# Moving the result matmuls to the head of the values loop, and halving the last quarters on VectorE, in a decode-attention kernel

## The chip, the cores and the metric

The kernel runs on one core of a Trainium2 chip. The metric is the device time in microseconds (us) of one execution. Most runs of one kernel agree within a few tenths of a microsecond. Kernels are compared only within the same rounds. A "ratio" is the mean time of one kernel's fast runs over the mean of the other's fast runs of the same rounds, so it is not quite the ratio of the medians quoted beside it.

## The reference

```python
B, H, Sq, Skv, Dh = 8, 32, 1, 4096, 128          # q, k, v in bf16
scores = jnp.einsum('bhqd,bhkd->bhqk', q, k) * Dh ** -0.5
attn = jax.nn.softmax(scores, axis=-1)
out = jnp.einsum('bhqk,bhkd->bhqd', attn, v)
```

There are 256 heads with one query each. K and V are 268 MB each and every byte is used once. A tile is 8 heads: 128 partitions by 256 rows of 128 numbers, 8.39 MB. There are 32 tiles of K and 32 of V.

## The kernel before

For each tile t, VectorE multiplies K by the query and adds halves of the 128 columns together; TensorE adds up the columns that are left (matmuls with the identity), VectorE reduces the result to scores. ScalarE makes the weights. TensorE multiplies them with V in a loop one section later. The values of a tile stand in 32 rows and are picked out by four small matmuls ("result matmuls") and scaled.

```python
C, NT = 256, 32                     # rows per partition and tile; tiles
def width_of(t, lo):                # columns left for TensorE
    return D // 8 if lo == C // 2 and 0 < t < NT - 3 else D // 2

def product(t, lo, hi):
    # multiply by q, then, while more than width_of(t, lo) columns: add halves
...
def values_loop(t):
    with tc.tile_critical() as loop:           # TensorE alone, a While loop
        for i in range(EDGE):
            one(i, start=(i == 0), stop=False)
        ...                                    # 10 rounds of 6 matmuls
        for i in range(NV - EDGE, NV):
            one(i, start=False, stop=(i == NV - 1))
...
for t in range(NT):
    loop = 0 < t <= LT                         # LT = NT - 3 = 29
    ...
    product(t, 0, first)
    if 0 < t - 1 <= LT:
        if (t - 1) % R == 0:
            norm_of(n)
        if t > 1:
            result_of(t - 2)                   # four matmuls
    if t + 2 < NT:
        q_prep(t + 2)
    if loop:
        sum_over_d(t, 0, HALF)
        product(t, HALF, C)
        sum_over_d(t, HALF, C)
        scores_of(t, 0, HALF)
        ...
        values_loop(t - 1)
        load("k", t + 1)
        load("v", t)
        scores_of(t, HALF, C)
    else:
        ...                                    # quarters instead of halves
```

K and V share three buffers. K of tile t+1 takes the buffer that the loop over V of tile t-2 leaves; V of tile t takes the buffer of K of tile t once its sums are done. So the end of a loop releases the next issue of K, and the end of the sums the next issue of V.

## Time and profile before

| | before |
|---|---|
| median of 3 runs | 1250.9 us (1250.84 to 1250.91) |
| span of the profiled run | 1249.5 us |
| DMA queue of K and V, share of the span | 99.5% |
| VectorE busy | 81% |
| TensorE busy | 61% |
| time from one landing to the next, mid-run | 19.35 us for 8.39 MB |

How to read it: no compute engine is full and the queue is. The lines are in the prediction, with what each shows.

### The profile page before, as it was taken

The numbers are of one execution on the slowest core, as the hardware profiler recorded it, in microseconds if no ns is written. First come the engines' busy times: TensorE is split into PE (matmuls) and PEld (weight loads), VectorE is DVE, ScalarE is ACT, GpSimd is POOL, SyncE is SP. The second block draws the span as 40 slices with busy tenths as digits, with TensorE's granted clock in tenths as the row PEclk, the third lists the DMA queues.
The fourth block names the chain that finished last, engine by engine and source line by source line (L and its number), as shares of the span: only waits on it lengthen the run. The fifth ranks groups of instructions, "written<-read, shape, count | busy, mean of one in ns | idle before, by whom it ended". The sixth has DMA issues, their size and how long they took to land. (4 is left out here: it accounts for less than half of the span.)

```text
span 1249.5 us, 10534 instructions
## 1 busy us (share of the span) xinstructions
PE 761.4 (61%) x3004; PEld 284.3 (23%) x3004; DVE 1010.6 (81%) x379; ACT 166.1 (13%) x433; POOL 4.5 (0%) x24
## 2 busy tenths in 40 slices
PE   3356457554586555766557665577655676556855
PEld 1122122221222212222122222122221222212312
DVE  7877987778977789777797777987779877798694
ACT  0111011111011110111101111011110111101111
POOL 1000000000000000000000000000000000000000
PEclk9786798777887777878678777887867877778867
DMA  9999999999999999999999999999999999999998
GB/s 405 436 436 435 436 429 424 426 436 437 436 432 435 435 434 434 435 435 426 431 436 435 426 430 436 435 434 437 433 432 430 433 437 432 433 432 425 429 442 339
DMA packets 11430, 537.30 MB, mean 430 GB/s; under 512 B 1808, under 2 KB 2064, under 8 KB 2320
## 3 DMA queue, kind: packets, MB, share of 16 engines
q1 hardware_dynamic: 11072, 536.94, 99.5%
q8 instruction: 14, 0.23, 0.1%
q10 hardware_dynamic: 336, 0.07, 0.0%
q14 instruction: 8, 0.07, 0.0%
HBM read 536.94 MB, written 0.07 MB: 430 GB/s over the span
## 5 line engine op out<-in xcount | busy, mean ns | idle before, releaser
L189 DVE TENSOR_TENSOR kt<-kt,qb 128x16384 bf16<-128x16384 bf16 (+1 forms) x70 | 556.8, 7955 | 156.8 <-DMA kt<-in_k_dram 150.1
L207 PE MATMUL ps<-kt,ident 128*128 128x512 bf16 x688 | 253.2, 537 | 416.3 <-DVE kt L195 415.9
L290 PE MATMUL av<-vt,w 128*32 x1740 | 425.3, 397 | 4.4
L195 DVE TENSOR_TENSOR kt<-kt 128x4096 bf16<-128x4096 bf16 (+1 forms) x126 | 382.7, 3037 | 4.3
L290 PEld LDWEIGHTS av<-vt,w 128*32 x1740 | 173.3, 100 | 262.1 <-issue 118.9
L207 PEld LDWEIGHTS <-ident 128*128 128x128 bf16 x688 | 80.0, 125 | 583.0 <-DVE kt L195 444.7
L244 ACT ACTIVATE e<-sc,nmax 128x256 bf16<-128x256 f32 x32 | 16.2, 508 | 708.0 <-DVE nmax L238 708.0
L251 ACT ACTIVATE w<-e,mine 128x256 bf16<-128x256 bf16 x256 | 105.6, 495 | 1.1
L219 DVE TENSOR_REDUCE sc<-ps 128x128 f32<-128x512 f32 (+1 forms) x70 | 48.1, 687 | 57.0 <-PE ps L207 57.0
L347 ACT ACTIVATE comb<-av 32x512 bf16<-32x512 f32 (+1 forms) x32 | 18.8, 586 | 327.3 <-PEq L280 320.9
L276 PE MATMUL av<-vt,w 128*32 128x512 bf16 x116 | 47.1, 498 | 14.5 <-issue 13.3
L367 PE MATMUL op<-comb,pick 32*16 32x128 bf16 (+1 forms) x128 | 12.2, 213 | 21.9 <-ACT comb L347 21.9
L276 PEld LDWEIGHTS av<-vt,w 128*32 128x32 bf16 x116 | 6.9, 101 | 54.7 <-issue 54.7
L175 PE MATMUL qp<-qg,heads 8*128 8x128 bf16 x32 | 7.0, 217 | 16.7 <-ACT qg L173 16.7
L367 PEld LDWEIGHTS <-pick 32*16 32x16 bf16 (+1 forms) x128 | 8.7, 83 | 28.9 <-issue 28.5
L231 DVE TENSOR_REDUCE pmax<-sc 128x1 f32<-128x256 f32 x32 | 13.4, 420 | 1.1
L318 PE MATMUL av<-vt,w 128*32 128x512 bf16 x188 | 13.7, 417 | 0.0
L173 ACT ACTIVATE qg<-qh 8x128 bf16<-8x128 f32 x32 | 8.5, 267 | 33.5 <-PE qh L169 33.5
L169 PE MATMUL qh<-q_all,ident 128*8 128x128 bf16 x32 | 7.2, 225 | 8.7 <-DMA q_all<-in_q_dram 8.3
L177 ACT ACTIVATE qb<-qp 128x128 bf16<-128x128 f32 x32 | 8.9, 278 | 9.7 <-PE qp L175 9.7
L339 DVE RECIPROCAL rz<-zp 16x1 f32<-16x1 f32 x16 | 2.3, 147 | 8.1 <-PE zp L332 8.1
L233 DVE TENSOR_SCALAR spread<-same,pmax 128x32 f32<-128x32 f32 x32 | 7.7, 242 | 1.1
(30 smaller groups left out, 45.7 us busy)
## 6 DMA issues: line engine op xcount, KB each, us to landing
kt<-in_k_dram SPq DMA_DIRECT2D x4, 4096.0 KB, 23.8
kt<-in_k_dram SPq DMA_DIRECT2D x4, 2048.0 KB, 12.3
vt<-in_v_dram SPq DMA_DIRECT2D x1, 4096.0 KB, 33.1
vt<-in_v_dram SPq DMA_DIRECT2D x1, 2048.0 KB, 37.6
vt<-in_v_dram SPq DMA_DIRECT2D x1, 1024.0 KB, 39.7
vt<-in_v_dram SPq DMA_DIRECT2D x1, 512.0 KB, 40.5
vt<-in_v_dram SPq DMA_DIRECT2D x31, 26.2
kt<-in_k_dram SPq DMA_DIRECT2D x29, 28.7
```

What stands on the lines that cost most here:

```text
L189: nc.vector.tensor_tensor(out=part, in0=part, in1=qb[:].to_broadcast([P, hi - lo, D]), op=ALU.mult)
L195: nc.vector.tensor_tensor(out=part[:, :, 0:n], in0=part[:, :, 0:n], in1=part[:, :, n : 2 * n], op=ALU.add)
L207: nc.tensor.matmul(ps[:], lhsT=ident[:], rhs=kt[:, lo:hi, s * ds : (s + 1) * ds], start=(s == 0), stop=(s == n - 1),)
L219: made = nc.vector.tensor_reduce(out=scs[t][:, lo:hi], in_=ps, axis=AX.X, op=ALU.add)
L231: nc.vector.tensor_reduce(out=pmax[:], in_=sc[:], axis=AX.X, op=ALU.max)
L244: nc.scalar.activation(out=e[:], in_=sc[:], func=ACT.Exp, bias=nmax[:, 0:1], scale=scale, accum_out=esums[t // R][:, t % R : t % R + 1],)
L251: nc.scalar.activation(out=w[:, :, g, :], in_=e_g, func=ACT.Copy, scale=mine[:, 0, g : g + 1])
L276: pe.matmul(av, lhsT=wf[:, i * nw : (i + 1) * nw], rhs=vf[:, i * nv : (i + 1) * nv], **how)
L290: pe.matmul(av, lhsT=wf[:, bass.ds(ow + i * nw, nw)], rhs=vf[:, bass.ds(ov + i * nv, nv)], start=False, stop=False,)
L318: nc.tensor.matmul(avs[t][j * AG : (j + 1) * AG, :], lhsT=w[:, i, :, :], rhs=vt[:, c0 : c0 + CB, :], start=(i < TG), stop=(j not in group[ ...
L347: nc.scalar.activation(out=comb[0:n, :, :], in_=av[0:n, :, :], func=ACT.Copy)
L367: nc.tensor.matmul(ops[n][:], lhsT=pick[0:e, m, r, :], rhs=comb[0:e, m, :], start=(r == 0 and m == 0), stop=(r == R - 1 and m == CB - 1 an ...
```

## The change

The intent: take TensorE work and a wait from in front of the first-half sums, and make the last tiles' scores come sooner by giving their last quarters' additions to VectorE.

```diff
+    LT = NT - 3
 ...
     def width_of(t, lo):
-        return D // 8 if lo == C // 2 and 0 < t < NT - 3 else D // 2
+        if t == 0:
+            return D // 2
+        return D // 8 if lo == (C // 2 if t <= LT else 3 * C // 4) else D // 2
 ...
         with tc.tile_critical() as loop:
+            if t > 0:
+                result_of(t - 1)
             for i in range(EDGE):
                 one(i, start=(i == 0), stop=False)
 ...
                 if (t - 1) % R == 0:
                     norm_of(n)
-                if t > 1:
+                if t > LT:
                     result_of(t - 2)
```

The rest of the diff renames a variable and moves `LT` up.

More of the change, by code (lines that the diff above doesn't have):

```diff
@@ L299, in values_loop @@
         loops.append(loop)
-    LT = NT - 3
     def values_of(t, lo, hi):
@@ L397 @@
         for t in range(NT):
-            loop = 0 < t <= LT
+            halves = 0 < t <= LT
             v_last = t >= NT - 2
             n = t // R - 1
-            if not loop:
+            if not halves:
                 if t + 1 < NT:
@@ L404 @@
                 load("v", t)
-            first = HALF if loop else Q
+            first = HALF if halves else Q
             product(t, 0, first)
-            if not loop:
+            if not halves:
                 sum_over_d(t, 0, first)
@@ L415 @@
                 q_prep(t + 2)
-            if loop:
+            if halves:
                 sum_over_d(t, 0, HALF)
@@ L440 @@
                 values_of(t - 1, 0, C)
-            if not loop:
+            if not halves:
                 scores_of(t, HALF + Q, C)
@@ L449 @@
                     store_of(n)
-                if not loop:
+                if not halves:
                     if t % R == 0:
```

## The prediction

> **What bounds the kernel now.** I read the busy shares first, then the DMA rows, then the waits, then one tile in the middle of the timeline, and last the end of the program. From the page:
>
> ```profile
> PE 761.4 (61%) x3004; PEld 284.3 (23%) x3004; DVE 1010.6 (81%) x379; ACT 166.1 (13%) x433; POOL 4.5 (0%) x24
> DMA  9999999999999999999999999999999999999998
> q1 hardware_dynamic: 11072, 536.94, 99.5%
> L189 DVE TENSOR_TENSOR kt<-kt,qb 128x16384 bf16<-128x16384 bf16 (+1 forms) x70 | 556.8, 7955 | 156.8 <-DMA kt<-in_k_dram 150.1
> vt<-in_v_dram SPq DMA_DIRECT2D x31, 26.2
> kt<-in_k_dram SPq DMA_DIRECT2D x29, 28.7
> ```
>
> No compute engine is full: VectorE, the busiest, is at 81%, and 150.1 us of its idle time is waiting for a K tile. The queue that carries K and V is busy 99.5% of the span. So the transfer is the suspect, and the question is whether it ever runs dry. One tile of the timeline answers that (start, duration, instruction):
>
> ```profile
> 618.16 0.33 SPq L156 DMA_DIRECT2D vt<-in_v_dram  x1
> 619.39 14.81 PE L290 MATMUL av<-vt,w 128*32 x60
> 625.12 8.69 DVE L189 TENSOR_TENSOR kt<-kt,qb 128x16384 bf16<-128x16384 bf16 x1 [5.29 <-DMA kt<-in_k_dram]
> 635.03 0.33 SPq L156 DMA_DIRECT2D kt<-in_k_dram  x1
> 635.67 0.38 PE L367 MATMUL op<-comb,pick 32*16 32x128 bf16 x4 [0.81 <-ACT comb L347]
> 638.33 5.32 PE L207 MATMUL ps<-kt,ident 128*128 128x512 bf16 x16 [1.57 <-DVE kt L195]
> ```
>
> A K tile lands just before 625.12, when VectorE's wait ends. The V tile was issued at 618.16, so 7 us before that; with the median of 26.2 us it lands at 644.4. The next K tile was issued at 635.03, which is 9.3 us before V lands; with its 28.7 us it lands at 663.7. So landings are at about 625.0, 644.4, 663.7: one each 19.35 us, and each transfer is queued 7 to 9 us before its predecessor is done. One tile is 128 x 256 x 128 x 2 bytes = 8.39 MB, and 8.39 MB / 19.35 us = 434 GB/s. The window of that period shows the same (last three numbers: TensorE clock, DMA share, GB/s):
>
> ```profile
> 625.00:663.70 38.70, 24.11 (x95) 9.15 (x94) 31.83 (x11) 5.03 (x13) 0.00 (x0) 0.78 1.00 434
> ```
>
> 64 such tiles at 19.35 us are 1238.4 us. The rest of 1249.5 is [...] some slower tiles, and what follows the last bytes.
>
> **The end.** The chain that ended last has V's transfer until 1245.48; then:
>
> ```profile
> 1242.30 3.09 PE L318 MATMUL av<-vt,w 128*32 128x512 bf16 x28
> 1245.53 0.83 PE L359 MATMUL op<-vt,w_last 128*16 128x128 bf16 x12
> 1246.19 0.39 PE L367 MATMUL op<-comb,pick 128*16 128x128 bf16 x4
> 1246.42 0.39 PE L359 MATMUL op<-vt,w_last 128*16 128x128 bf16 x4
> 1246.84 0.36 ACT L378 ACTIVATE stage<-op,rz 16x128 bf16<-16x128 f32 x1 [0.73 <-PE op L359]
> 1242.50:1245.00 2.50, 2.50 (x27) 1.05 (x26) 0.13 (x1) 0.00 (x0) 0.00 (x0) 0.81 0.60 224
> 1245.00:1247.50 2.50, 1.67 (x25) 1.18 (x20) 0.00 (x0) 0.96 (x2) 0.00 (x0) 1.00 0.11 39
> ```
>
> The first of the twelve at 1245.53 answers the landing of the eight-row piece of V at 1245.48, though the values matmuls before it had only just ended (1245.39). From there twenty small matmuls run without a gap, at (0.83 - 0.22) / 11 = 56 ns from one to the next (0.22 is the mean of one in the groups by line).
>
> [...] the trace swings between 0.50 and 1.00, and weight loads of the 512-column sums follow each other at 0.43 us in half-clock stretches.
>
> **The change part by part.** *A, result matmuls.* The order of instructions shows 28 groups of four (tiles 0 to 27) taken from in front of the query preparation and put in front of the values loop of the same section. Removed: a wait for the copy (16.6 us in all for 29 groups, about 0.6 each) and 0.38 us, per tile, between the loop's end and the first-half sums. These sums wait 1.57 us for VectorE anyway (the L207 row above), so taking some 1 us from in front of them moves nothing. Added: four 128-column matmuls before the loop, 4 x 56 ns = 0.22 us at full clock, or some 0.43 at half. The loop ends 0.2 to 0.4 us later, and so does the K issue that waits for it. Its 9.3 us of lead becomes about 9.0. V's issue waits for the sums, not the loop: unchanged. In odd sections the stage activation now also waits for the loop's end and stands before the copy there: +0.34 us on the copy and the query preparation after it, inside the same 1.57 us of slack together with the 1 us gained. Effect on the span: 0.
>
> *B, halving.* The diff's new width rule touches three tiles, not two. Tile 29 (the third last): its second half gets two more VectorE halvings, 2.29 + 1.23 = 3.5 us, and loses 12 of 16 sums at 0.43 = 5.1 us. V of tile 29 is issued about 1.5 us earlier than 1162.25. Tiles 30 and 31: the last quarter gets halvings of 2048 and 1024 elements, 1.23 + about 0.69 (estimate: 2292 - 1225 = 1067 ns for 2048 elements, so 1225 - 533) = 1.9 us, and loses 6 of 8 sums at 0.43 = 2.6 us. Net gain about 0.7 each. Summed with tile 29's, less A's 0.3: 1.5 + 0.7 + 0.7 - 0.3, so tile 31's last scores (1232.69) come about 2 us earlier (estimate, 1 to 2.5), and its first values at 1239.23 become some 1237.3. But V's pieces land when they land. The later value groups then wait for their pieces, and the twelve still begin at the 1245.48 landing. After it nothing is shorter: 12 + 4 + 4 matmuls, 0.36 us, the store. Effect: 0. Total VectorE +7.3 us, TensorE about -10 us, span 0.
>
> **The rivals.** *All hidden* (my choice): 1250.9. For it: every transfer has 6 us or more of lead, and the end is set by a landing. *The tail's clock falls back.* The values of tile 31 will come earlier and with holes between V's pieces, [...] twenty matmuls at 107 instead of 56 ns are +1.0 us: 1251.9. For it: the windows show 0.81 in the stretch just before, so it became full only there. [...] *The tail gains.* Values end earlier, so the copy at 1245.51 comes earlier: but the four that need it stand behind the twelve in TensorE's order and never waited for it. At most 0.2 us: 1250.7. *A new wait starves the DMA*: the loop would have to be over 9 us late, or V over 6; A adds 0.4 us. If it did by 1 us per tile, 28 us: 1279. I see no path. *Removed waits speed the middle*: only if transfers had gaps there; the 434 GB/s says not.
>
> **Range and chances.** Nothing in the middle moves; the tail gives -0.2 to +1.0. The three runs before lie within 0.07 us, but another chip or day may differ by some tenths (the profiled run took 1251.34). I take 1250.9, range 1250.1 to 1252.0. Over 2% would be 25 us either way: there is no such path down (it would need a faster DMA), and up only by starvation. Chances 0.005, 0.99, 0.005.
>
> **What would show each step right or wrong.** K issues with about 9 us lead, V with about 7, still 19.35 us per landing and 434 GB/s; the K wait of VectorE near 150 us; L367 gone from the place after the copy; VectorE's busy time +7, tile 31's last score some 2 us earlier, idle holes of TensorE between the last values; the end again V's landing, then some 1.3 us of matmuls. Wrong: a DMA share under 0.95 in mid-span windows, a granted clock of 0.5 after 1245 (then +1), or last values ending before and the twelve starting before V's piece has landed (impossible by the chain above).

The marked cuts are passages that no trace or run of this case shows. The forecast's sum is 1250.9 us (the median before) with 0 for part A and 0 for part B. In the rival of the falling clock the +1.0 us stands as an estimate: 20 x (107 - 56) ns, where 107 is a quarter of the 0.43 us by which weight loads of the 512-column sums follow each other at a granted clock of 0.50 (561.33 to 563.89 in the trace before; at 1.00, from 564.27, seven take 1.40 us). A clock that falls in a pause is seen in that trace too: TensorE's sums end at 643.65, the next start at 654.98, and the granted clock is 1.00 in the window from 643.65 to 646.13 and 0.50 from 646.13 to 654.97. Of the start the trace shows that the first packet of K comes at 1.82 us.

## More of the kernel before

The page lists queues 8 and 14 too, as of the kind `instruction`:

```profile
q8 instruction: 14, 0.23, 0.1%
q14 instruction: 8, 0.07, 0.0%
```

The columns are packets, MB and the share of the 16 DMA engines' time. Such a packet is called an instruction fetch below.

## The result, and the profile after

| | before | after |
|---|---|---|
| median of 6 runs each | 1250.9 us (1250.77 to 1251.86) | 1251.51 us (1251.27 to 1252.11) |
| ratio | | 1.0004, interval 0.9991 to 1.0017 |
| span of the profiled run | 1249.5 us | 1249.7 us |

The time is the same, as predicted, and within the range. Yet five of six runs before lie at or under 1250.91, and all six after at or over 1251.27: there is a small thing of about 0.6 us that the prediction has at 0.

The page after, busy times and the queue of instructions:

```profile
PE 744.1 (60%) x2980; PEld 288.4 (23%) x2980; DVE 1017.9 (81%) x385; ACT 163.2 (13%) x433; POOL 4.4 (0%) x24
q14 instruction: 9, 0.07, 0.0%
```

VectorE has six instructions and 7.3 us more, TensorE 24 fewer matmuls. And there is one packet of queue 14 more. One tile in the middle of the timeline after (start, duration, instruction):

```profile
617.78 0.33 SPq L157 DMA_DIRECT2D vt<-in_v_dram  x1
618.20 0.59 PE L370 MATMUL op<-comb,pick 32*16 32x128 bf16 x4 [0.45 <-issue]
618.72 1.03 PE L279 MATMUL av<-vt,w 128*32 128x512 bf16 x2
624.76 8.69 DVE L191 TENSOR_TENSOR kt<-kt,qb 128x16384 bf16<-128x16384 bf16 x1 [5.30 <-DMA kt<-in_k_dram]
635.01 0.33 SPq L157 DMA_DIRECT2D kt<-in_k_dram  x1
637.97 3.63 PE L209 MATMUL ps<-kt,ident 128*128 128x512 bf16 x16 [1.70 <-DVE kt L197]
```

The result matmuls now stand at 618.20, in front of the loop, which starts 0.52 us later (618.72 less 618.20). The first-half sums still wait for VectorE, 1.70 us instead of 1.57. VectorE still waits 5.3 us for K. Nothing in the middle moved, and the window of the same stretch gives the same rate:

```profile
625.00:663.70 38.70, 22.55 (x94) 9.12 (x93) 31.83 (x12) 5.17 (x14) 0.00 (x0) 0.82 1.00 434
```

The end of the timeline after, from TensorE's values of tile 31 on, and the windows there (clock, DMA share and GB/s at the right):

```profile
1241.40 1.89 PE L321 MATMUL av<-vt,w 128*32 128x512 bf16 x16 [2.28 <-DMA vt<-in_v_dram]
1243.88 0.61 PE L321 MATMUL av<-vt,w 128*32 128x512 bf16 x8 [0.59 <-DMA vt<-in_v_dram]
1245.10 0.40 PE L321 MATMUL av<-vt,w 128*32 128x512 bf16 x4 [0.61 <-DMA vt<-in_v_dram]
1245.75 0.83 PE L362 MATMUL op<-vt,w_last 128*16 128x128 bf16 x12 [0.25 <-DMA vt<-in_v_dram]
...
1247.06 0.36 ACT L381 ACTIVATE stage<-op,rz 16x128 bf16<-16x128 f32 x1 [0.86 <-PE op L362]
1242.50:1245.00 2.50, 1.41 (x15) 0.48 (x11) 0.00 (x0) 0.00 (x0) 0.00 (x0) 1.00 0.51 193
1245.00:1247.50 2.50, 1.68 (x24) 1.19 (x23) 0.00 (x0) 0.96 (x2) 0.00 (x0) 1.00 0.06 17
```

Where 28 values matmuls ran as one stretch before, each group now waits for its piece of V: the scores came sooner and the gain became waiting. The end is again a landing: the eight-row piece landed at 1245.71, and the twelve start at 1245.75. Before, that piece landed at 1245.48. So what came later is V itself, by 0.23 us in this pair of traces. (The profiled run of the kernel before took 1251.34 us, 0.4 more than its median, and its K of tile 31 landed late, as the next paragraph shows. That hides part of the difference in this pair.)

Following the landings back (issue plus time to landing), one transfer stands out. K of tile 31 landed at 1207.04 before and 1206.59 after. V of tile 30, which follows it in the queue, was issued at 1199.45 before and 1197.78 after. Its time to landing, from the view of that instruction, before and then after:

```profile
DMA to landing us min/median/max: 27.0/27.0/27.0
```

```profile
DMA to landing us min/median/max: 28.9/28.9/28.9
```

It landed at 1226.44 and at 1226.71: 19.40 us after K before, 20.12 us after K now. A transfer that was earlier in the queue took 0.7 us longer. In just that stretch, 1207 to 1222 us, the DMA view of the changed kernel has a packet that the kernel before does not have there:

```profile
q14 instruction: 1, 0.01, 0.1%
```

In the packet records of the trace this is 8192 bytes at 1215.6 us. The DMA engine that carries it (found by its packets, each of which starts where the one before ends) is held up: the packet takes 0.33 us and the next 64 KB packet behind it 3.08 instead of 2.42 us, 0.97 us in all. No other 64 KB packet between 1200 and 1232 us takes over 2.6 us in that trace. The trace has a record for each of the 16 parts of a load, and the landing quoted here is the last of them: after, 15 parts of V of tile 30 are there by 1225.95 us and the last one at 1226.71; before, the last two come at 1226.39 and 1226.44. In the trace before, the ninth packet of queue 14 comes at 1250.9, after the last instruction.

Not every fetch costs something. The kernel before has a 16 KB packet of queue 8 at 1219.6 us, also while V of tile 30 is on its way (after: 1223.7), and V still takes 19.40 us. Of its 55 whole-tile transfers between 81 and 1149 us, 16 had a fetch in their stretch (from the landing ahead to their own). Six of these took 19.56 to 20.65 us; the other ten took 19.47 us or less, as did all 39 without a fetch. For V of tile 30 the packet records show the difference. Before, its parts came over 3.4 us (1223.08 to 1226.44). The engine with the 16 KB packet lost 1.55 us there (1.08 until the next 64 KB packet starts, which takes 2.89 instead of 2.42) and ended its last 64 KB of the tile at 1226.01; without the loss that is 1224.46 (estimate). After, the engine with the 8 KB packet ended at 1226.24, and the last part is there 0.47 us later; without the 0.97 us the part is there at 1225.74 (estimate), only 0.21 us ahead of the last of the other 15. So of these two fetches one was absorbed on an engine that was ahead, and one was not, on an engine among the last. The other transfers with a fetch were not looked at in this way.

So the first theory is: **the six added VectorE instructions pull an instruction fetch from after the end into the run, and it holds up V.** The rivals: the later K issue (0.4 us per tile) costs the 0.6 us; or the new timing of the last tiles does, whatever the number of instructions.

### The profile page after: what moved, and what is told of

It reads as the page before. It is cut to its first block, busy times and chain, and to the rows that moved or that the text cites. A ratio compares the mean times of both kernels' runs of the same rounds, so it can differ in the third digit from the quotient of the medians.

```text
span 1249.7 us, 10496 instructions
## 1 busy us (share of the span) xinstructions
PE 744.1 (60%) x2980; PEld 288.4 (23%) x2980; DVE 1017.9 (81%) x385; ACT 163.2 (13%) x433; POOL 4.4 (0%) x24
## 5 line engine op out<-in xcount | busy, mean ns | idle before, releaser
L209 PE MATMUL ps<-kt,ident 128*128 128x512 bf16 x664 | 228.7, 507 | 444.2 <-DVE kt L197 443.9
L295 PE MATMUL av<-vt,w 128*32 x1740 | 430.8, 413 | 0.3
L197 DVE TENSOR_TENSOR kt<-kt 128x8192 bf16<-128x8192 bf16 (+2 forms) x132 | 390.0, 2955 | 4.5
L295 PEld LDWEIGHTS av<-vt,w 128*32 x1740 | 183.0, 105 | 254.0 <-issue 86.7
L209 PEld LDWEIGHTS <-ident 128*128 128x128 bf16 x664 | 72.6, 118 | 600.7 <-DVE kt L197 479.8
L370 PE MATMUL op<-comb,pick 32*16 32x128 bf16 (+1 forms) x128 | 18.1, 289 | 15.6 <-issue 12.6
L381 ACT ACTIVATE stage<-op,rz 16x128 bf16<-16x128 f32 x16 | 5.7, 357 | 162.9 <-PEq L283 162.0
L370 PEld LDWEIGHTS op<-comb,pick 32*16 32x16 bf16 x112 | 8.7, 109 | 38.0 <-issue 38.0
L233 DVE TENSOR_REDUCE pmax<-sc 128x1 f32<-128x256 f32 x32 | 13.4, 420 | 1.1
L321 PEld LDWEIGHTS <-w 128*32 128x32 bf16 x188 | 6.3, 112 | 12.3 <-issue 9.5
```

The source lines that it names most:

```text
L197: nc.vector.tensor_tensor(out=part[:, :, 0:n], in0=part[:, :, 0:n], in1=part[:, :, n : 2 * n], op=ALU.add)
L209: nc.tensor.matmul(ps[:], lhsT=ident[:], rhs=kt[:, lo:hi, s * ds : (s + 1) * ds], start=(s == 0), stop=(s == n - 1),)
L233: nc.vector.tensor_reduce(out=pmax[:], in_=sc[:], axis=AX.X, op=ALU.max)
L295: pe.matmul(av, lhsT=wf[:, bass.ds(ow + i * nw, nw)], rhs=vf[:, bass.ds(ov + i * nv, nv)], start=False, stop=False,)
L321: nc.tensor.matmul(avs[t][j * AG : (j + 1) * AG, :], lhsT=w[:, i, :, :], rhs=vt[:, c0 : c0 + CB, :], start=(i < TG), stop=(j not in group[ ...
L370: nc.tensor.matmul(ops[n][:], lhsT=pick[0:e, m, r, :], rhs=comb[0:e, m, :], start=(r == 0 and m == 0), stop=(r == R - 1 and m == CB - 1 an ...
```

## The experiments

Twelve kernels were run, in three groups, each group on one chip with its own runs of the kernel before. Medians of before were 1250.90, 1250.94 and 1250.98 us, 9 runs in each group, 1250.74 to 1251.19 over all. "Span" is the median, over the timed runs, from the first to the last instruction; the time has some 1.7 to 2.2 us more than the span. "q14" is the number of queue 14's packets on the page.

| kernel | median us (range) | ratio | span us | q14 |
|---|---|---|---|---|
| before, per group | 1250.90 to 1250.98 | 1 | 1249.0 to 1249.1 | 8 |
| e1, result matmuls alone | 1250.86 (1250.82 to 1251.45) | 0.9999 | 1249.0 | 8 |
| e2, tile 29's halving alone | 1251.12 (1250.84 to 1251.19) | 1.0002 | 1249.4 | 8 |
| e3, last two tiles' halving alone | 1251.33 (1251.30 to 1251.53) | 1.0004 | 1249.6 | 9 |
| e4, the whole change again | 1251.61 (1251.43 to 1251.99) | 1.0006 | 1249.8 | 9 |
| e10, before + six idle VectorE instructions | 1251.52 (1251.26 to 1251.93) | 1.0004 | 1249.8 | 10 |
| e11, after, eight instructions to GpSimd | 1251.27 (1251.19 to 1251.61) | 1.0003 | 1249.1 | 8 |
| e12, after, eight instructions fewer | 1251.26 (1251.12 to 1251.34) | 1.0002 | 1249.2 | 8 |
| e7, last quarters not halved | 1251.10 (1251.05 to 1251.25) | 1.0001 | 1249.05 | 8 |
| e5, each loop some 3 us longer | 1252.22 (1252.14 to 1252.77) | 1.0011 | 1250.45 | 9 |
| e6, each loop some 13 us longer | 1376.89 (one look) | | 1375.2 | 9 |
| e8, light V, before | 1156.81 (1155.43 to 1158.90) | 0.9253 | 1154.9 | 8 |
| e9, light V, after | 1164.93 (1164.78 to 1165.80) | 0.9314 | 1163.2 | 9 |

### The parts one by one (first group)

**e1**, the result matmuls alone:

```diff
 # after, with the old rule
-        if t == 0:
-            return D // 2
-        return D // 8 if lo == (C // 2 if t <= LT else 3 * C // 4) else D // 2
+        return D // 8 if lo == C // 2 and 0 < t < NT - 3 else D // 2
```

> Part A alone: the result matmuls at the head of the loop, the old widths. Theory (all hidden under the K and V transfers): within 0.3 us of before, ratio 1.0000 +- 0.0003; K issued some 0.3 to 1 us later, still over 8 us before the transfer ahead of it has landed. Rival (the +0.6 us of the changed kernel's median is A's: later K issues): ratio 1.0005, about 1251.5 us. Second rival (the wait removed in front of the first-half sums is worth something): 28 x 0.6 = 17 us faster.

Measured: 1250.86 us. All hidden holds; both rivals fall. K's lead is 8.2 us at the least (landing and issue records, 26 tiles in mid-run). The result matmuls cost nothing and save nothing that these runs show.

**e2**, the halving of tile 29 alone, and **e3**, that of tiles 30 and 31 alone:

```diff
 # e2: before, with
-        return D // 8 if lo == C // 2 and 0 < t < NT - 3 else D // 2
+        return D // 8 if lo == C // 2 and 0 < t < NT - 2 else D // 2
 # e3: before, with
+        if t >= NT - 2:
+            return D // 8 if lo == 3 * C // 4 else D // 2
```

> The third last tile's wider halving alone. Theory: V of tile 29 is issued about 1.5 us earlier, no time gained: within 0.3 us of before. Rival (the +0.6 us comes from the last tiles' new timing): it would show here or in the next run as +0.5 us.

> The halving of the last quarters of the last two tiles alone. Theory: tile 31's last score comes about 1 us earlier, the values then wait for V's pieces, the end stays V's landing: within 0.3 us of before. Rival: the finishing values gain, -0.5 us or more[...].

Measured: e2 1251.12 us, within the 0.3 us, but its profiled run (1250.84) was its fastest, and whether its slower runs had a fetch more is not known. e3 1251.33 us, all five runs over every run of before in that group: it is 0.43 us over before where 0.3 were expected at most, so the theory "no time" misses. V of tile 30 landed 19.96 us after K in e3, 19.49 in e2 and 19.44 in e1.

**e4**, the whole change once more, unedited:

> The whole change once more, on the same chip as the three parts. Theory (the 0.6 us between the medians is no cost of one part but differences of single transfers): ratio between 0.9997 and 1.0005. Rival (a real cost of about 0.6 us): ratio 1.0005 again with an interval that excludes 1.

Measured: 1251.61 us, every run (1251.43 to 1251.99) over every run of before (1250.77 to 1251.17). The ratio's interval, 0.9992 to 1.0019, includes 1, but the ranges do not overlap: the difference of 0.7 us is real, and the theory of chance falls. V of tile 30 took 20.11 us again.

### Is it the instruction fetch? (second and third group)

**e10** adds instructions and no work:

```diff
 # before
+    idle = consts.tile([P, 6], F32, name="idle")
+    for i in range(6):
+        nc.vector.memset(idle[:, i : i + 1], 0.0)
```

> The kernel before, with six one-column memsets on VectorE at the very start, before its first K has landed; nothing else. Theory (the halving of the last two tiles costs its 0.4 us not by what it does but because its instructions pull one more 8 KB instruction fetch into the run, at 1215 us of the trace, which holds up one DMA engine by about 1 us while it carries V of tile 30): the packet of queue 14 appears near 1215 us, V of tile 30 lands 20.0 to 20.2 us after K of tile 31 instead of 19.4, and the median is 1251.3 to 1251.5. Rival (the new timing of the last scores and values costs it): 1250.9 and no such packet.

Measured: 1251.52 us, and V of tile 30 landed 20.32 us after K, both a little over the expected ranges (the profiled run, 1251.93, was the slowest of the five). Again one part came late: 15 by 1225.93, the last at 1227.15. Six memsets of one column, done before the first K has landed, cost what the whole change costs. The page of e10:

```profile
q14 instruction: 10, 0.07, 0.0%
```

Of the two more one is 8 KB at 1216.0 us, the other 40 bytes at the start (packet records). The rival, the timing of the last scores, falls as the cause of these 0.6 us: e10 does not touch them.

**e11** gives eight instructions of the changed kernel to GpSimd, **e12** leaves eight out:

```diff
 # e11: after, with
-        nc.vector.tensor_scalar(
+        (nc.gpsimd if 2 <= t < 10 else nc.vector).tensor_scalar(
             out=spread[:], ...
 # e12: after, with
+        if 2 <= t < 10:      # the bias is then 0: right for these scores
+            nc.vector.tensor_reduce(
+                out=nmax[:], in_=same[:], axis=AX.X, op=ALU.max, apply_transpose=True
+            )
+        else:
+            ...              # spread, then nmax, as before
```

> The whole change, with eight of VectorE's small instructions (the spread of the maximum, tiles 2 to 9) given to GpSimd, so that VectorE's stream is no longer than before. Theory (instruction fetch): the packet near 1215 us is gone, V of tile 30 lands within 19.5 us, median 1250.8 to 1251.1. Rival (the timing of the last tiles): still 1251.5.

> The whole change, with eight VectorE instructions taken out and none given to another engine: for tiles 2 to 9 the spread of the maximum is skipped and the bias is taken from the mask, which is 0 (the scores are small, so the result stays right). Theory (one more instruction fetch is the whole cost of the change): the packet near 1215 us is gone, V of tile 30 lands within 19.5 us, median 1250.8 to 1251.1; the 0.3 us that the run with GpSimd kept were GpSimd's. Rival (a second cost of 0.3 us remains in the change): 1251.2 to 1251.4 again.

Measured: the packet is gone in both (the page of e12):

```profile
q14 instruction: 8, 0.07, 0.0%
```

That the fetches are VectorE's shows in their times: those at 541.3 and 902.7 before came sooner with instructions added (512.2 and 890.7 in e10) and later with instructions taken out (553.1 and 931.4 in e12). V of tile 30 lands 19.36 and 19.34 us after K, and the span is back at before's: 1249.1 and 1249.2 against 1249.1 (1249.7 to 1249.8 for the changed kernel). But the time only went to 1251.27 and 1251.26, not to 1250.8 to 1251.1: both miss their range by some 0.2 us. GpSimd is not the reason, since e12 gives it nothing. What is left lies outside the span: the time less the span is 2.20 and 2.06 us in these two, 1.83 and 1.84 in before of the same rounds, 1.75 in the changed kernel. e7, below, has 2.05 with two VectorE instructions fewer than before. The record does order this stretch, by the number of VectorE instructions (first row of each page). The last fetch of queue 14, which stands after the last instruction in these kernels, moves with it:

| VectorE instructions | kernels | last fetch ends after the span, us (traces) | time less span, us (medians) |
|---|---|---|---|
| 377 | e7, e11, e12 | 2.05 to 2.14 | 2.05 to 2.20 |
| 379 | before, e1 | 1.60 to 1.65 | 1.83 to 1.87 |
| 381 | e2 | 0.86 | 1.77 |
| 383, 385 | e3, after, e4, e10 | inside the span | 1.71 to 1.76 |

So e11 and e12 did not go back to before's 379 instructions but to two fewer, and in their traces the last fetch ends some 0.4 to 0.5 us later after the span than before. That it makes the time longer was not shown: this is an ordering of few traces that was seen afterwards, and no run was made to test it.

### Does the end hang on V alone? (second group)

**e7** does the reverse of the change in the last quarters of the last two tiles:

```diff
 # before, with
+        if t >= NT - 2 and lo == 3 * C // 4:
+            return D
```

> The reverse of the change's second part: before, with the last quarters of the last two tiles not halved at all, so VectorE has 2.3 us less and TensorE 3.4 us more for each. Theory (before had only about 0.1 us to spare at the end, its last values end 1245.39 and V's piece lands 1245.48): tile 31's scores come 2 us later and the end follows by 1 to 2 us, about 1252.4. Rival (the end hangs on V's landing alone, whatever the values do): 1250.9.

Measured: 1251.10 us, so the theory (1252.4) misses and the rival is nearer. The reason is in the clock. The last sums of tile 31, before and then in e7:

```profile
1229.06 3.60 PE L207 MATMUL ps<-kt,ident 128*128 128x512 bf16 x8 [3.72 <-DVE kt L195]
```

```profile
1225.19 3.63 PE L209 MATMUL ps<-kt,ident 128*128 128x512 bf16 x16 [1.39 <-DVE kt L191]
1245.06 0.83 PE L361 MATMUL op<-vt,w_last 128*16 128x128 bf16 x12 [0.20 <-DMA vt<-in_v_dram]
```

Sixteen sums took as long as eight: 0.23 us each against 0.45. The eight ran at half clock (granted 0.50 in the window of 1229.06 to 1232.66 before). The sixteen ran at the rate of full clock: in the changed kernel sixteen take the same 3.63 us from 637.97, at a granted 1.00. I had priced the eight added sums at half clock, 3.4 us. So tile 31's scores came sooner, not later, and the twelve began 0.04 us after the landing of their piece (1245.02) as in the traces before (0.05) and after (0.04). What e7 does not tell is how late the scores may come, since it did not make them late.

### How far is TensorE's work hidden? (second and third group)

**e5** and **e6** put copies of the loop's first matmul in front of each loop; the real one overwrites them:

```diff
 # after, with 14 (e5) or 65 (e6)
+            for _ in range(14):
+                one(0, start=True, stop=True)
             for i in range(EDGE):
                 one(i, start=(i == 0), stop=False)
```

> The whole change with 14 more copies of the loop's first matmul in front of each of 29 loops, overwritten by the real one: 3 to 5 us more before K's issue in each tile, ten times what the moved result matmuls add. Theory (K's issue has 9 us of lead): lead falls to 4 to 6 us, transfers stay 19.35 us apart, time within 0.5 us of the changed kernel's 1251.5. Rival (TensorE time in front of the loop is on the path): 29 x 4 = 116 us slower.

> As the run with 14 copies, but 65 of them: 14 to 17 us more in front of each loop, more than K's issue has of lead (9 us). Theory (the lead is what hides TensorE's work, and it ends): two tiles then take sums 33 + loop 16.5 + 14 to 17 + transfer of one K 21.4 = 85 to 88 us instead of 77.4, so 4 to 5 us more for each of 28 tiles: 1350 to 1400 us, and the transfers are no longer 19.35 us apart. Rival (TensorE's time is hidden whatever it is): 1252 to 1254.

Measured: e5 1252.22 us. From V's issue to K's it is 20.2 us in the mean, 2.9 more than in the changed kernel and just under the expected 3 to 5. K's issue of the tile shown above moved from 635.01 to 638.35, its lead over the transfer ahead of it is mostly 5.2 to 7 us now, transfers stay 19.35 us apart and the rival's 116 us are not there. Yet it is 0.7 us over the changed kernel, just over what was expected. The 14 x 29 more instructions brought three more fetches of queue 8 (17 instead of 14), and the last of them falls into the end, in the DMA view of 1240 to 1247 us:

```profile
q8 instruction: 1, 0.02, 1.0%
```

The packet records put these 16 KB at 1244.7. A fetch at the end is nothing new: the kernel before has one at 1243.3 (the same line in that view) and the changed kernel one at 1245.1. But here the piece of V that lands 0.32 us after the one ahead of it before, and 0.35 after, took 1.34 us: 15 of its parts are there by 1245.90, the last at 1246.91. TensorE waited for it. That the place of the fetch costs, and not only the number, is my reading of these records; which engine carried the late part was not followed here:

```profile
1245.61 0.61 PE L364 MATMUL op<-vt,w_last 128*16 128x128 bf16 x8 [0.25 <-DMA vt<-in_v_dram]
1246.95 0.39 PE L364 MATMUL op<-vt,w_last 128*16 128x128 bf16 x4 [0.73 <-DMA vt<-in_v_dram]
```

e6 took 1376.89 us (one look, state unknown), inside the expected 1350 to 1400; each loop was 13.4 us longer (median), a little under the 14 to 17. The lead was used up: VectorE starts a K tile at 603.83 and the next but one at 688.10, 84.3 us for two tiles, where 85 to 88 had been worked out from the loop of K issue, K transfer, products, sums and values loop. Two lines show it, VectorE's wait for K and a window of two tiles:

```profile
603.83 8.69 DVE L191 TENSOR_TENSOR kt<-kt,qb 128x16384 bf16<-128x16384 bf16 x1 [14.32 <-DMA kt<-in_k_dram]
600.00:685.00 85.00, 70.35 (x321) 30.28 (x320) 63.72 (x23) 10.09 (x27) 0.00 (x0) 0.92 0.92 393
```

The same wait for K that meant "the transfers bound" before is there, longer, where the transfers do not bound any more: the rate, 393 instead of 434 GB/s, tells the two apart.

### What would the result matmuls be worth without the bound? (third group)

**e8** (before) and **e9** (after) load only 112 of V's 256 columns for tiles 0 to 28 and walk over them in smaller steps. The result is wrong; the instructions are the same.

```diff
-        for n in cuts.get((kind, t), [C]):
+        for n in cuts.get((kind, t), [C if kind == "k" or t > LT - 1 else 112]):
 ...
-                pe.reg_add(rv, rv, LOOP * nv)
+                pe.reg_add(rv, rv, 2 * nv)
```

> Before, with only 112 of 256 columns of V loaded for tiles 0 to 28, the values loop going over them in smaller steps (a wrong result on purpose; the same instructions). A tile's transfers are then 12.1 MB, 27.8 us, and VectorE's chain of 33.5 us a tile should bound the middle: 1251 - 28 x 5.2 = about 1105 us. This is the ground for the next run.

> The whole change with V as light as in the run before. Theory (the moved result matmuls cost and save nothing because the sums behind them wait for VectorE, not only because the transfers bound): within 2 us of the run before. Rival (the wait of 0.6 us in front of the first-half sums is worth something once the transfers do not bound): 17 us faster than it.

Measured: 1156.81 and 1164.93 us. The first is 50 us slower than expected: not VectorE's 33.5 us a tile bound it, but the same loop as in e6, about 35 us a tile: a K issued at 588.54 lands at 610.25, its sums let V be issued at 642.14, and the values loop behind them lets a K be issued at 659.14, 70.6 us for two tiles. VectorE starts a K tile at 610.37 and the next at 645.44, and waits for K though the rate is only 340 GB/s there (window of 600 to 670 us of e8):

```profile
600.00:670.00 70.00, 44.84 (x184) 17.37 (x184) 63.22 (x24) 10.32 (x27) 0.00 (x0) 0.82 0.81 340
645.44 8.69 DVE L190 TENSOR_TENSOR kt<-kt,qb 128x16384 bf16<-128x16384 bf16 x1 [1.63 <-DMA kt<-in_k_dram]
```

And both the theory (within 2 us) and the rival (17 us faster) miss: the changed kernel is 8.1 us slower. The head of the values loop in e8, then in e9:

```profile
642.14 0.33 SPq L157 DMA_DIRECT2D vt<-in_v_dram  x1
642.66 1.04 PE L278 MATMUL av<-vt,w 128*32 128x512 bf16 x2 [0.55 <-issue]
```

```profile
647.36 0.33 SPq L157 DMA_DIRECT2D vt<-in_v_dram  x1
647.87 0.59 PE L371 MATMUL op<-comb,pick 32*16 32x128 bf16 x4 [0.55 <-issue]
648.39 1.04 PE L280 MATMUL av<-vt,w 128*32 128x512 bf16 x2
```

From V's issue to the loop's first matmul it is 0.52 us before and 1.03 us after, 0.51 more. The values loop and the K issue behind it come round once in two tiles, so 28 tiles x 0.51 / 2 = 7.1 us of the 8.1 are accounted for (an estimate). The runs of e8 scatter by 3.5 us, so no more can be asked of the difference.

## Why the prediction was right, and where it was not

- **The bound.** Right: 434 GB/s before and after, 19.35 us from landing to landing, leads of about 7 us for V. K's lead stayed mostly between 8.1 and 10 us (predicted 9). The smallest lead of a whole V tile before was 5.9 us (tile 29), just under the "6 us or more" of the prediction.
- **Part A, effect 0.** Right (e1: 1250.86 us). The loop's end came later as predicted, "0.2 to 0.4 us": its first matmul starts 0.52 us later, but from V's issue to K's it is 16.88 us before and 17.27 after (means of 26 tiles), 0.39 more, and K's mean lead goes from 9.43 to 9.04 us. The reason given, "Its 9.3 us of lead becomes about 9.0", is the right one: e5 takes 2.9 us more of that lead with transfers unmoved, e6 takes more than there is and pays 125 us. That the sums "wait 1.57 us for VectorE anyway" holds too (1.70 us). e9 adds what the prediction did not say: where the lead is gone, the moved matmuls stand on the path, and moving them is a loss.
- **Part B, the last scores "about 2 us earlier".** Right: the last score reduction moved from 1232.69 to 1230.46, the first values from 1239.23 to 1237.00 (predicted 1237.3), and the gain became holes of 2.28, 0.59 and 0.61 us. But the price of a sum, 0.43 us, holds at half clock alone; in e7 it was 0.23 us in the same place. By these two the change's gain for the scores is worth less when the clock is full there (estimate). TensorE's total was mis-sized too: its busy time fell by 17.3 us, not by about 10.
- **The end.** Right: the twelve start 0.04 us after the piece lands, and 1.28 us of matmuls follow. The rival of the falling clock did not come: 1.00 in both windows. The hole of 2.28 us did not lower it here.
- **"V's pieces land when they land", effect 0.** This is the step that missed its size. They landed later, since six more VectorE instructions brought one more instruction fetch into the run; predicted 0 for part B, found about 0.6 us for the whole (1251.51 less 1250.9; 0.7 us in e4's rounds). That the time still fell into the stated range is owed to its upper side, 1252.0, which was there for another cause, the falling clock. No rival named it: all of them were about waits and clocks, and none about what else the DMA engines carry. That the fetch and not the halving costs it is shown by e10 (six idle instructions, the same cost) and, for the span, by e11 and e12 (the fetch gone, the span back). A rest of 0.3 us in e11 and e12 lies outside the span; it goes with the last fetch, but no run shows that as its cause. Why the added fetch falls on an engine that is among the last is open.

No version beat the kernel before: e1 is level with it. Fewer instructions are no simple remedy: e7, e11 and e12 have two VectorE instructions fewer than before and medians 0.16 to 0.33 us above it.

## What to carry to other kernels

Ask of each wait whether the thing waited for was itself late: here VectorE waits 150 us for K, but each transfer is queued 7 to 9 us before the one ahead has landed, so what is left to move the middle is bytes, or what else rides on the DMA engines. In such a kernel count instructions as traffic: when a change that should be hidden costs half a microsecond, look at when the packets of the instruction queues come, and whether one part of a load lands long after the other 15. The number of fetches alone does not tell the cost: in the kernel before, ten of 16 transfers with a fetch were on time. Work that is hidden by a lead is not free; measure the lead before you spend it (here 3 us were hidden and 13 us cost 125).
